# Windowed attention with a gated FFT convolution on one core: gate factors copied out by ScalarE, the inverse's sums as single steps, and an order of work from perturbed priorities

## The chip, the core and the metric

The kernel runs on one core of one Trainium2 chip. The number that counts is the device time of one execution in microseconds; of the kernel before there are three runs, with a median of 190.96 us (190.31 to 191.09). The profile shows one more execution, which took 190.2 us, of which the span from its first to its last instruction is 188.4 us. Engines are named as the profile names them: PE does the matmuls (PEld its weight loads), ACT is ScalarE, DVE is VectorE, POOL is GpSimd, which here issues most of the loads, and SP issues the rest of the loads and all stores.

## The reference

There are 4 batches of 768 positions, 8 heads of width 64, and a model width of 512. The first half is causal attention over a window of 96 positions plus 8 global positions that every row sees, with a linear bias by distance. The second half multiplies two projections of the attention's output with an FFT convolution of a third one.

```python
# attention, for each batch and head
keep   = (pos_k < 8) | ((rel >= 0) & (rel < 96))          # rel = pos_q - pos_k
scores = q @ k.T / 8 - slope[h] * dist                     # dist: rel, or 96 for the global ones
a      = softmax(where(keep, scores, -1e9))
x      = concat_heads(a @ v)                               # 768 x 512
# gate and convolution, for each batch
x1, x2, x3 = split(x @ w_proj, 3)                          # each 768 x 512
conv   = irfft(rfft(x2, axis=0) * rfft(filter, axis=0))    # along the 768 positions
out    = (x1 * conv * x3) @ w_out
```

## The kernel before

**Attention.** Keys lie in 7 tiles of 120 rows with the 8 global rows in front of each. `transposes` brings q and k into the layout that the matmuls want (tiles `QT`, `KT`; line 714, copied out at line 386). The 7 key tiles are worked in 3 chunks c = 0, 1, 2. `scores` makes one chunk's scores for a pair of heads (line 751), ACT takes the exponential of them from two PSUM banks (line 765, tile `E`, 48 times in all), and DVE multiplies with a mask that holds the bias (line 772). For batch 0 the bias can instead be added by PE, by matmuls of `near` with `slope` ahead of the scores (line 742, one or two for each score matmul); then no mask is multiplied. `NEAR = 3` says that this holds for chunks 0, 1 and 2 of batch 0. `values` multiplies with v (lines 790 and 795), DVE takes the reciprocal of the row sums (`rc`, line 819), and `xn` is the scaled result: either one DVE instruction (line 814) or 8 or 12 small ACT instructions (line 818). `transpose_x` turns it into `xT` (line 835).

**Gates.** `gate(b, j, s)` makes 128 columns j of one half s of x1 and x3 for batch b: 8 matmuls into two banks (line 873). The first bank is copied out and scaled to fp16 (tile `x`, line 390 on ACT or 392 on DVE); DVE then multiplies the second bank, still fp32 in PSUM, with it (tile `g`, line 881). There are 32 gates.

**Convolution.** `butterfly` folds x along the positions on DVE (`xab`, `xcf`, `xo`, `xr`, lines 849 to 860), `conv` projects (line 922, copied out to `ab`), transforms (line 700, copied out to `X`), multiplies with the filter's spectrum (`prod`, lines 1039 to 1046), and transforms back (lines 944 and 947, copied out to `eo`, line 386). `mixed` then makes three sums in place on DVE, five instructions (lines 988 to 992) as one step of the plan; `gated` joins the halves (lines 1009, 1010) and multiplies by the gate (line 1014, tile `y`); the last projection is line 970 and its copy-out `ot`.

**What sets the order.** Nothing is issued as the code stands. Each step is recorded in a `Plan` with a cost for each engine that may run it, its reads and writes, and the PSUM banks it takes. `schedule` then plays the steps out once: again and again it takes the step that can start first by the plan's costs, and between steps that can start within 0.03 of each other the one with the smaller key, which is the step's batch, its place in the batch and a bias. Where a step may run on ACT or DVE, the one that ends it first by the costs gets it. The result is a fixed order for each engine; on the chip each engine goes through its own list in that order and waits where a semaphore says so. `fill` puts idle matmuls (tile `idle`, line 382) where the plan leaves PE free for long.

```python
key = lambda o: o.batch[0] + o.batch[1] * o.tail / (total[o.batch] or 1.0) + o.bias
```

Of the kernel before, what the change touches and what calls it, by code (L numbers as in the profile page):

```python
# [13 lines left out]
Alu = mybir.AluOpType  # L14
# [12 lines left out]
def act(n):  # L27
    return 0.06 + n / 1200.0
# [31 lines left out]
class Op:  # L60
    __slots__ = ("cost", "fn", "preds", "succs", "wait", "tail", "bias", "acq", "use", "n",
                 "start", "end", "ready", "eng", "bytes", "batch", "table", "name", "order", "first", "landed")


class Plan:
# [54 lines left out]

    def schedule(self):
        for o in self.ops:
            for x in o.preds:
                x.succs.append(o)
            o.ready = 0.0
        self.before = {}
# [5 lines left out]
        for o in self.ops:  # L132
            o.first = set()
            for b in o.acq:
                for u in b.users:
                    o.first |= self.outer(u, {o}, o)
            o.first -= o.preds | {o}
            o.wait = len(o.preds) + len(o.first)
        after = {}
        for o in self.ops:  # L140
            for x in o.first:
                after.setdefault(x, []).append(o)
        total = {}
        for o in self.ops:
            o.tail = total.get(o.batch, 0.0)
            total[o.batch] = o.tail + o.cost.get("P", 0.0)
        free = {e: BEGIN for e in "PAVGS"}
        banks = [0.0] * 8
# [3 lines left out]
        out = []  # L152
        key = lambda o: o.batch[0] + o.batch[1] * o.tail / (total[o.batch] or 1.0) + o.bias
        while live:
            best = None
            for o in live:
                at = o.ready
                where = None
                if o.acq:
                    if len(o.acq) == 2:  # L160
                        i = min(range(0, 8, 2), key=lambda i: max(banks[i], banks[i + 1]))
                        where = (i, i + 1)
                    else:
                        first = max(at, min(banks))
                        where = [max((i for i in range(8) if banks[i] <= first),
                                     key=lambda i: (banks[i ^ 1], banks[i], -i), default=0)]
# [5 lines left out]
                got = (s, key(o), o, e, where)  # L172
# [37 lines left out]
        self.span = max(o.end for o in out)  # L210
        return self.program(self.fill(out))

    BUSY = 0.225
    FAVOUR = 0.0

# [77 lines left out]
class Fused:  # L293
    PERIOD = 40.0
    NEAR = 3
    LATER = ()
# [251 lines left out]
    def distances(self):  # L548
# [33 lines left out]
        for half in range(2):  # L582
            for k in range(2):
                src, dst = dg[64 * k:64 * k + 64], near[64 * half:64 * half + 64, k]

                def spread(e, src=src, dst=dst):
                    self.copy(e, dst[:, 0:n], src[:, 0:n])
                    self.copy(e, dst[:, n:2 * n + 48], src)
                g.op("AV", {"A": act(216) + act(264), "V": dve(216, 4) + dve(264, 4)}, spread,
                     r=["dg"], w=[("near", half, k)], bias=-2900, name="near")  # L590
# [4 lines left out]
        for half in range(2):  # L595
            ps = slice(64 * half, 64 * half + 64)
            for hp in range(4):
                dst = self.slope[ps, hp].rearrange("p k c -> p (k c)")
                dst = dst[:, 0:256].rearrange("p (k c) -> p k c", k=2)
                for k in range(2):  # L600
                    g.op("AV", {"A": act(64), "V": dve(64, 2)}, lambda e, ps=ps, hp=hp, k=k: self.times(
                        e, self.slope[ps, hp, k, 64 * k:64 * k + 64], self.ident[ps, ps],
                        self.slopes[2 * hp + ps.start // 64] / self.scale),
                        r=["ident", "slope"], w=[("slope", half, hp, k)], bias=-2950, name="slope")

    def masks(self):
        g, nc, NL, n = self.g, self.nc, self.NL, 216
        v, dg, far, mask = nc.vector, self.dg, self.far, self.mask
        for hp in range(4):
# [13 lines left out]
            g.op("V", 2 * dve(400, 4) + 2 * dve(216, 4), spread, r=["far"] + [  # L623
                ("mask", h, at) for h in (2 * hp, 2 * hp + 1) for at in (n, 600)],
# [150 lines left out]
    def values(self, j, c, slot):  # L775
# [34 lines left out]
        def scaled(e):  # L810
# [5 lines left out]
            for i in range(2):  # L816
                for n in range(2 * nt):
                    nc.scalar.mul(to[:, i, n], o[:, i, n, 0:D], rc[:, i, n])  # L818
        g.op("V", 0.09 + 0.05 * nt, lambda _: nc.vector.reciprocal(rc, view()[:, :, :, D:D + 1]),
             use=bs, w=[key], name="rc")  # L820
        g.op("AV", {"A": 4 * nt * act(D), "V": dve(4 * nt * D, 1, True)}, scaled, use=bs, r=[key],
             w=[("xn", j, c)], name="xn")
# [40 lines left out]
    def gate(self, b, j, s):  # L863
# [4 lines left out]
        for o in (0, 2 * self.DM):  # L868
            bk = g.bank()

            def run(_, o=o, bk=bk):
# [8 lines left out]
             use=[pts[0]], w=[key], name="x1")  # L880
        g.op("V", dve(h, 1, True), lambda _: nc.vector.tensor_mul(  # L881
            gt[:, j, h * s:h * s + h], pts[1].f32()[:, 0:h], x1), use=[pts[1]], r=[key],
            w=[("g", b % 2, j, s)], name="g")

# [97 lines left out]
    def mixed(self, js):  # L982
# [3 lines left out]

        def run(_):
            v.tensor_sub(t, z, u)
            v.tensor_scalar(u, u, 2.0, None, op0=Alu.mult)
            v.tensor_add(z, z, u)  # L990
            v.tensor_sub(u, t, w)
            v.tensor_add(w, t, w)
        self.g.op("V", 4 * dve(512 * n, 2) + dve(512 * n, 4), run, name="mix", w=[
            ("mixed", jp) for jp in js] + [
            ("eo", jp, jj, par) for jp in js for jj in range(2) for par in range(2)])

    def gated(self, b, jps, half):
# [8 lines left out]
        def join(_):  # L1006
# [4 lines left out]
        ys = [("y", jp, half) for jp in jps]  # L1011
        g.op("V", dve(512 * n, 2) + dve(256 * n, 2), join, r=[("mixed", jp) for jp in jps] + [
            ("eo", jp, jj, par) for jp in jps for jj in range(2) for par in range(2)], w=ys, name="half")
# [69 lines left out]
    def first_rows(self, vt):  # L1083
# [4 lines left out]
        rows = vt[0:NG, :, :, 0:self.D]  # L1088
        self.g.op("AV", {"A": act(512), "V": dve(512, 2)}, lambda e: self.copy(e, rows[:, 0], st),
                  r=[("X", 0)], w=[("vng", 0, 0, 0)], name="vfirst")  # L1090
# [93 lines left out]
```

## Time and profile before

| what | value |
|---|---|
| median of 3 runs | 190.96 us (190.31 to 191.09) |
| the profiled execution: time, span | 190.2 us, 188.4 us |
| granted PE clock | 1.00 |
| PE busy | 174.0 us, 92% of the span |
| DVE busy | 166.1 us, 88% |
| ACT busy | 144.0 us, 76% |
| POOL busy, all of it before 90 us | 76.6 us, 41% |
| DMA | 20.47 MB |

Three engines are busy most of the time, so the shares alone don't say which one counts. They have to be read stage by stage, and together with the chain of waits. "Busy" counts an instruction from its start to its end: on ACT and DVE the next one often starts before the last has ended, so the step from start to start, called pitch here, is what one more instruction costs. A pitch is read from a row that holds several instructions.

### The profile page before, as it was taken

What the parts mean: (1) busy time and instruction counts of PE and PEld (TensorE: products, weight loads), DVE (VectorE), ACT (ScalarE), POOL (GpSimd) and SP (SyncE); (2) the same over time, 40 slices, a digit from 0 to 9 for tenths busy, and PEclk for the clock granted to TensorE, in tenths of its full rate; (3) what the DMA queues carried; (4) which work ended last, traced back from release to release, by engine and by line L of the source; (5) the groups of instructions that cost most, each with busy time, mean ns of one, the idle gap of its engine ahead of it and who ended that gap; (6) DMA issues with size and microseconds to landing.
All of it is one profiled execution on the core that took longest, in us unless ns stands there. A gap on an engine that the chain in (4) does not pass through costs nothing.

```text
span 188.4 us, 4561 instructions
## 1 busy us (share of the span) xinstructions
PE 174.0 (92%) x1742; PEld 105.7 (56%) x1742; DVE 166.1 (88%) x378; ACT 144.0 (76%) x292; POOL 76.6 (41%) x97
## 2 busy tenths in 40 slices
PE   7877999999899999899898999999998999999891
PEld 2345886656445667575355567754466675447440
DVE  6898875998999969999997869999999999999960
ACT  7389983568999999988967669859869576588352
POOL 8799993599989999993000000000000000000000
PEclk9999999999999999999999999999999999999999
DMA  6999999999999999999053000000260000005244
GB/s 134 197 167 149 153 196 209 154 153 152 143 171 145 154 141 140 142 151 132 4 220 117 0 3 0 3 0 2 80 257 1 5 0 0 3 29 194 111 165 169
DMA packets 90916, 20.47 MB, mean 109 GB/s; under 512 B 83816, under 2 KB 87824, under 8 KB 90896
## 3 DMA queue, kind: packets, MB, share of 16 engines
q0 software_dynamic: 80912, 12.14, 95.6%
q1 hardware_dynamic: 9984, 8.06, 13.6%
q8 instruction: 13, 0.21, 0.5%
q14 instruction: 7, 0.06, 0.1%
HBM read 25.84 MB, written 6.29 MB: 171 GB/s over the span
## 4 chain that ended last, share of the span: by engine, by line
DVE 42%; PE 32%; ACT 13%; issue 4%; SPq 4%; DMA 3%; DVEq 0%; ACTq 0%
PE bank L873 13%; PE bank L970 5%; DVE E L772 4%; SPq L402 4%; DVE g L881 4%; ACT E L765 4%; DMA ot<-in_q_dram 3%; DVE xn L814 3%; DVE y L1014 3%; PE bank L922 2%; PE bank L944 2%; DVE pp L1039 2%; ACT xn L818 2%; ACT QT L386 2%; PE bank L790 2%
## 5 line engine op out<-in xcount | busy, mean ns | idle before, releaser
L873 PE MATMUL bank<-xT,w 128*128 128x384 f16 x256 | 45.0, 326 | 0.2 <-ACT xT L386 0.2
L765 ACT ACTIVATE E<-bank 128x864 f16<-128x864 f32 x48 | 40.1, 910 | 1.2 <-PE bank L751 0.6
L873 PEld LDWEIGHTS <-w 128*128 128x128 f16 x256 | 24.3, 98 | 16.3 <-issue 1.3
L402 POOL DMA_DIRECT2D kn<-in_k_dram x28 | 26.6, 960 | 0.7 <-issue 0.5
L402 POOL DMA_DIRECT2D vn<-in_v_dram x28 | 25.6, 928 | 2.5 <-DMA w<-in_moe_w_proj_dram 1.9
L390 ACT ACTIVATE x<-bank 128x384 f16<-128x384 f32 x29 | 14.7, 508 | 12.7 <-PE bank L873 10.5
L970 PE MATMUL bank<-wo,y 128*128 128x512 f16 x96 | 21.9, 379 | 1.1 <-DVE y L1014 1.0
L772 DVE TENSOR_TENSOR E<-E,mask 128x864 f16<-128x864 f16 x36 | 20.5, 594 | 1.2 <-ACT E L765 1.1
L881 DVE TENSOR_TENSOR g<-bank,x 128x384 f16<-128x384 f32 x32 | 17.1, 549 | 3.9 <-PE bank L873 3.6
L390 ACT ACTIVATE ot<-bank 128x512 f32<-128x512 f32 x21 | 12.5, 597 | 8.2 <-PE bank L970 8.1
L402 POOL DMA_DIRECT2D qn<-in_q_dram x18 | 16.2, 910 | 5.0 <-DMA g<-in_moe_filter_fft_dram 3.5
L751 PE MATMUL bank<-QT,KT 64*128 64x216 f16 (+2 forms) x224 | 15.8, 241 | 2.0 <-ACT E L765 0.9
L970 PEld LDWEIGHTS <-y 128*128 128x128 f16 x96 | 9.0, 98 | 13.1 <-DVE y L1014 3.1
L790 PE MATMUL bank<-vn,E 128*128 128x65 f16 x224 | 15.5, 193 | 0.9 <-ACT E L765 0.8
L814 DVE TENSOR_TENSOR xn<-bank,rc 128x512 f16<-128x512 f32 (+1 forms) x21 | 16.1, 771 | 0.2
L390 ACT ACTIVATE ab<-bank 128x512 f16<-128x512 f32 x21 | 12.5, 611 | 4.0 <-PE bank L922 3.9
L790 PEld LDWEIGHTS <-E 128*128 128x128 f16 x224 | 14.0, 97 | 2.6 <-DVE E L772 0.7
L795 PE MATMUL bank<-vn,E 128*128 128x65 f16 x192 | 15.2, 193 | 0.0
L386 ACT CAST eo<-bank 128x384 f16<-128x384 f32 x29 | 12.9, 509 | 1.7 <-PE bank L947 1.2
L751 PEld LDWEIGHTS <-KT 64*128 64x128 f16 x224 | 8.5, 94 | 9.2 <-issue 5.8
L386 ACT CAST X<-bank 128x512 f16<-128x512 f32 x21 | 11.9, 606 | 2.2 <-PE bank L700 2.1
L795 PEld LDWEIGHTS <-E 128*128 128x128 f16 x192 | 13.2, 97 | 0.6 <-issue 0.3
(141 smaller groups left out, 361.6 us busy)
## 6 DMA issues: line engine op xcount, KB each, us to landing
out_dram<-ot SPq DMA_DIRECT2D x24, 256.0 KB, 2.6
kn<-in_k_dram POOLq DMA_DIRECT2D x28, 120.0 KB, 6.0
vn<-in_v_dram POOLq DMA_DIRECT2D x28, 120.0 KB, 6.7
qn<-in_q_dram POOLq DMA_DIRECT2D x18, 128.0 KB, 6.7
ot<-in_q_dram SPq DMA_DIRECT2D x6, 256.0 KB, 5.8
w<-in_moe_w_proj_dram POOLq DMA_DIRECT2D x4, 256.0 KB, 6.6
g<-in_moe_filter_fft_dram POOLq DMA_DIRECT2D x1, 768.0 KB, 11.9
w<-in_moe_w_proj_dram POOLq DMA_DIRECT2D x1, 512.0 KB, 8.6
```

What stands on the lines that cost most here:

```text
L386: {"A": nc.scalar.copy, "V": nc.vector.tensor_copy, "G": nc.gpsimd.tensor_copy}[e](out, in_)
L390: self.nc.scalar.mul(out, in_, c)
L402: return self.g.op(eng, 0.57 + 0.00035 * nbytes[0] if eng == "G" else 0.5, lambda _: e.dma_start(dst, src), w=w, r=r, nbytes=nbytes, name= ...
L751: nc.tensor.matmul(bs[hh].f32()[:, off:off + w], self.KT[hs, hp, P * m:P * m + P], self.QT[hs, hp, KL * m:KL * m + w], start=(off == 0 and ...
L765: g.op("A", act(864), lambda _: nc.scalar.activation(eo, bs[0].two()[:, :, 0:432].rearrange("p h (m w) -> p h m w", m=2), Act.Exp, scale=s ...
L772: g.op("V", dve(864, 2), lambda _: nc.vector.tensor_mul(eo, eo, mk), r=[("E", hp, gi), ("mask", hp)], w=[("E", hp, gi)], name="masked")
L790: nc.tensor.matmul(o[:, n, hh], ef[:, at:at + P], vt[:, t, 2 * hp + hh, :], start=first, stop=(t == 0), skip_group_check=True)
L795: nc.tensor.matmul(o[:, n, hh], ef[:, at:at + P], vt[:, t - 1, 2 * hp + hh, :], start=False, stop=True, skip_group_check=True)
L814: nc.vector.tensor_mul(to, o[:, :, :, 0:D], rc.to_broadcast([P, 2, 2 * nt, D]))
L873: nc.tensor.matmul(bk.f32()[:, 0:h], self.w[:, c, o + P * j:o + P * j + P], self.xT[:, c, h * s:h * s + h], start=(c == 0), stop=(c == 3))
L881: g.op("V", dve(h, 1, True), lambda _: nc.vector.tensor_mul(gt[:, j, h * s:h * s + h], pts[1].f32()[:, 0:h], x1), use=[pts[1]], r=[key], w ...
L970: nc.tensor.matmul(bk.f32(), y[:, c, P * t:P * t + P], self.wo[:, c, :], start=(c == 0), stop=(c == 3))
```

## The change

- **Gates.** For all 32 gates (`TWICE`) ACT copies the second bank, x3, out to fp16 in the tile `g` (new line 920); DVE then multiplies `g` with x1 from SBUF to SBUF (new line 922).
- **The inverse's sums.** The five instructions of `mixed` are five steps of the plan, so that other DVE work can be put between them, and `gated` waits for the three that it reads.
- **`NEAR` is 2.** Chunk 2 of batch 0 gets its bias by the mask on DVE and no longer by PE.
- **Costs.** Some costs in the plan are other numbers: the casts of q, `near`, the mask's `spread`, `rc`, and `xn` on ACT (4 x 0.2 for each tile in place of 4 x 0.113). The copies of `slope` are for ACT alone.
- **Order.** Before the play-out, 25 seeds each shift the key of some steps by a random amount (`noise`) and their leaning towards ACT or DVE (`lean`).

```diff
     def schedule(self):
+        self.prepare()
+        for seed in self.SEEDS:
+            self.shake(seed)
+        return self.program(self.fill(self.lay()))
+
+    def shake(self, seed):
+        r = random.Random(seed)
+        if r.random() < 0.4:
+            groups = sorted({(o.name, o.batch) for o in self.ops if o.eng not in "GS"})
+            g, by = r.choice(groups), r.gauss(0.0, 5.0)
+            lean = r.gauss(0.0, 0.3)
+            for o in self.ops:
+                if (o.name, o.batch) == g:
+                    o.noise += by
+                    o.lean += lean
+            return
+        share = r.choice((0.005, 0.02, 0.05))
+        for o in self.ops:
+            if r.random() < share:
+                o.noise += r.gauss(0.0, 5.0)
+                o.lean += r.gauss(0.0, 0.3)
...
+            o.rank = o.batch[0] + o.batch[1] * o.tail / (total[o.batch] or 1.0) + o.bias + o.noise
...
-                           key=lambda x: (x[1] + o.cost[x[0]] + self.FAVOUR * (x[0] == "V"), x[0]))
+                           key=lambda x: (x[1] + o.cost[x[0]] + o.lean * (x[0] == "V"), x[0]))
...
+    SEEDS = (4, 6, 12, 14, 28, 33, 52, 54, 91, 94, 109, 172, 179, 217, 284, 340, 370, 416, 512,
+             1076, 1771, 1829, 3912, 4133, 4161)
...
-    NEAR = 3
+    NEAR = 2
+    TWICE = frozenset((b, j, s) for b in range(4) for j in range(4) for s in range(2))
...
-            self.g.op("AV", {"A": act(512), "V": dve(512, 2)}, lambda e: self.copy(
+            self.g.op("AV", {"A": act(512), "V": 0.7}, lambda e: self.copy(
...
-                    g.op("AV", {"A": act(64), "V": dve(64, 2)}, lambda e, ps=ps, hp=hp, k=k: self.times(
+                    g.op("A", {"A": 0.145}, lambda e, ps=ps, hp=hp, k=k: self.times(
...
-        g.op("AV", {"A": 4 * nt * act(D), "V": dve(4 * nt * D, 1, True)}, scaled, use=bs, r=[key],
+        g.op("AV", {"A": 4 * nt * 0.2, "V": dve(4 * nt * D, 1, True)}, scaled, use=bs, r=[key],
...
+        x3, ko = gt[:, j, h * s:h * s + h], ("g", b % 2, j, s)
+        if (b, j, s) in self.TWICE:
+            g.op("A", act(h), lambda _: nc.scalar.copy(x3, pts[1].f32()[:, 0:h]), use=[pts[1]],
+                 w=[ko], name="x3")
+            g.op("V", dve(h, 2), lambda _: nc.vector.tensor_mul(x3, x3, x1), r=[key], w=[ko], name="g")
+            return
...
-        def run(_):
-            v.tensor_sub(t, z, u)
-            v.tensor_scalar(u, u, 2.0, None, op0=Alu.mult)
-            v.tensor_add(z, z, u)
-            v.tensor_sub(u, t, w)
-            v.tensor_add(w, t, w)
...
+        op(lambda _: v.tensor_sub(t, z, u), (), "mt")
+        op(lambda _: v.tensor_scalar(u, u, 2.0, None, op0=Alu.mult), ("mt",), "mu", 4)
+        op(lambda _: v.tensor_add(z, z, u), ("mt", "mu"), "mz")
+        op(lambda _: v.tensor_sub(u, t, w), ("mt", "mu", "mz"), "m1")
+        op(lambda _: v.tensor_add(w, t, w), ("mt", "m1"), "m2")
```

How the instructions move is shown at three places, word for word from the built programs' orders. Line numbers of the changed kernel are 37 to 42 higher; `bank` with a number is a pair of PSUM banks.

**ACT at the start, up to the first exponentials.** `ot` here holds the loaded rows of q in fp32, and `ot_104` the last of the six tiles. Before:

```order
L612 ACTIVATE mask<-dg 128x48
L612 ACTIVATE mask<-dg 128x216
L386 CAST qn<-ot_103 128x512
L386 COPY QT<-bank_122 128x4x128
L386 CAST qn<-ot_104 128x512
L765 ACTIVATE E_67<-bank_123 128x2x2x216
L765 ACTIVATE E_68<-bank_124 128x2x2x216
```

Now:

```order
L423 CAST qn<-ot_102 128x512
L423 COPY QT<-bank_121 128x4x128
L649 ACTIVATE mask<-dg 128x48
L423 CAST qn<-ot_103 128x512
L423 COPY QT<-bank_121 128x4x128
L802 ACTIVATE E_68<-bank_123 128x2x2x216
L802 ACTIVATE E_67<-bank_124 128x2x2x216
```

The cast of the sixth tile of q no longer stands ahead of the exponentials (it is DVE's), while four other casts that DVE had are ACT's.

**ACT at the first gates of batch 0.** Before:

```order
L390 ACTIVATE x_95<-bank_123 128x384
L390 ACTIVATE x_96<-bank_121 128x384
L390 ACTIVATE x_97<-bank_122 128x384
L390 ACTIVATE x_98<-bank_123 128x384
L494 ACTIVATE y<-bank_123 128x512
```

Now (`g_87 <- bank` is the new copy of x3):

```order
L427 ACTIVATE x_95<-bank_124 128x384
L427 ACTIVATE x_96<-bank_122 128x384
L920 CAST g_87<-bank_123 128x384
L427 ACTIVATE x_97<-bank_123 128x384
L920 CAST g_87<-bank_124 128x384
L920 CAST g_87<-bank_122 128x384
L920 CAST g_87<-bank_121 128x384
```

Seven copies stand where four were, and the pair of banks of a gate is freed by ACT alone.

**DVE at the end of batch 2's inverse**, where the fold for batch 3 is made as well. Before:

```order
L856 TENSOR_TENSOR xo<-xab,xcf 128x1024
L988 TENSOR_TENSOR mix<-eo 128x1024
L989 TENSOR_SCALAR eo<-eo 128x8x128
L990 TENSOR_TENSOR eo<-eo 128x8x128
L991 TENSOR_TENSOR eo<-mix,eo 128x8x128
L992 TENSOR_TENSOR eo<-mix,eo 128x8x128
```

Now:

```order
L1033 TENSOR_TENSOR mix<-eo 128x1024
L886 TENSOR_TENSOR xab<-xT 128x1536
L888 TENSOR_TENSOR xab<-xT 128x1536
L1034 TENSOR_SCALAR eo<-eo 128x8x128
L891 TENSOR_TENSOR xcf<-xab 128x1024
L892 TENSOR_TENSOR xcf<-xab 128x1024
L1035 TENSOR_TENSOR eo<-eo 128x8x128
L893 TENSOR_TENSOR xo<-xab,xcf 128x1024
L1036 TENSOR_TENSOR eo<-mix,eo 128x8x128
```

The five sums stood back to back, each touching a tile that the one ahead of it reads or writes; now work of the fold stands between them.

More of the change, by code (lines that the diff above doesn't have):

```diff
@@ L61 @@
     __slots__ = ("cost", "fn", "preds", "succs", "wait", "tail", "bias", "acq", "use", "n",
-                 "start", "end", "ready", "eng", "bytes", "batch", "table", "name", "order", "first", "landed")
+                 "start", "end", "ready", "rank", "noise", "lean", "need", "eng", "bytes", "batch", "table", "name", "order", "first", "landed")
 class Plan:
@@ L124, in schedule @@
                 x.succs.append(o)
-            o.ready = 0.0
+            o.noise, o.lean = 0.0, self.FAVOUR
+            o.eng = next(iter(o.cost))
         self.before = {}
@@ L137, in schedule @@
             o.first -= o.preds | {o}
-            o.wait = len(o.preds) + len(o.first)
-        after = {}
+            o.need = len(o.preds) + len(o.first)
+        self.after = {}
         for o in self.ops:
             for x in o.first:
-                after.setdefault(x, []).append(o)
+                self.after.setdefault(x, []).append(o)
         total = {}
@@ L146, in schedule, with lay @@
             total[o.batch] = o.tail + o.cost.get("P", 0.0)
+        self.total = total
+    def schedule(self):
+        self.prepare()
[18 more added lines that the diff above has]
+                o.lean += r.gauss(0.0, 0.3)
+    def lay(self):
+        for o in self.ops:
+            o.wait, o.ready = o.need, 0.0
+            for b in o.acq:
+                b.left, b.free = 1 + len(b.users), 0.0
+        total, after = self.total, self.after
         free = {e: BEGIN for e in "PAVGS"}
@@ L152, in schedule @@
         out = []
-        key = lambda o: o.batch[0] + o.batch[1] * o.tail / (total[o.batch] or 1.0) + o.bias
+        for o in self.ops:
+            o.rank = o.batch[0] + o.batch[1] * o.tail / (total[o.batch] or 1.0) + o.bias + o.noise
         while live:
@@ L985, in mixed, with op @@
         z, u, w = (eo[:, :, :, P * m:P * m + P] for m in range(3))
-        def run(_):
[L988 to L995, printed above, removed]
+        def op(fn, r, w, rate=2):
+            self.g.op("V", dve(512 * n, rate), fn, name="mix", r=[("eo", jp, jj, par) for jp in js
+                      for jj in range(2) for par in range(2)] + [(k, jp) for k in r for jp in js],
+                      w=[(w, jp) for jp in js])
+        op(lambda _: v.tensor_sub(t, z, u), (), "mt")
[3 more added lines that the diff above has]
+        op(lambda _: v.tensor_add(w, t, w), ("mt", "m1"), "m2")
     def gated(self, b, jps, half):
```

22 lines of the change are left out of this document (11 added, 11 removed).

## The prediction

> **What bounds the kernel now.** I cut the span at the first projection matmul (line 922) of each batch, which the trace puts at 41.9, 85.5, 127.4 and 156.3 us, and asked for the busy time of each engine in the five stretches: batch 0's attention, three mixed stages, and the end.
>
> ```profile
> 0.00:41.90 41.90, 37.73 (x447) 24.49 (x448) 34.44 (x107) 28.78 (x66) 34.44 (x51) 1.00 1.77 168
> 41.90:85.50 43.60, 41.09 (x451) 26.02 (x449) 40.56 (x91) 41.41 (x85) 41.17 (x46) 1.00 2.46 149
> 85.50:127.40 41.90, 39.97 (x405) 24.16 (x402) 37.27 (x74) 32.76 (x70) 1.00 (x2) 1.00 0.31 52
> 127.40:156.30 28.90, 28.13 (x298) 17.71 (x299) 28.35 (x56) 22.93 (x41) 0.00 (x0) 1.00 0.15 56
> 156.30:188.40 32.10, 27.09 (x149) 13.27 (x146) 25.47 (x56) 18.11 (x35) 0.00 (x0) 1.00 0.26 99
> ```
>
> The columns are length, PE, PEld, DVE, ACT, POOL. The reader sees that PE is busy 94 to 97% in the middle three, DVE 93, 89 and 98%, ACT 95, 78 and 79%. PE's number flatters it, since its ends are modelled; the chain of waits says who really ends last:
>
> ```profile
> DVE 42%; PE 32%; ACT 13%; issue 4%; SPq 4%; DMA 3%; DVEq 0%; ACTq 0%
> PE bank L873 13%; PE bank L970 5%; DVE E L772 4%; SPq L402 4%; DVE g L881 4%; ACT E L765 4%; DMA ot<-in_q_dram 3%; DVE xn L814 3%; DVE y L1014 3%; PE bank L922 2%; PE bank L944 2%; DVE pp L1039 2%; ACT xn L818 2%; ACT QT L386 2%; PE bank L790 2%
> L873 PE MATMUL bank<-xT,w 128*128 128x384 f16 x256 | 45.0, 326 | 0.2 <-ACT xT L386 0.2
> ```
>
> DVE carries 42% of it, so a us taken off DVE in the middle is worth most. ACT has room from 85.5 us on, little between 41.9 and 85.5. The kernel is not bound by one engine: whoever gets faster will soon wait for PE.
>
> **The gates.** The rows of the multiplication, of ACT's copies of the same shape (128x384 fp32 in PSUM to fp16), and of DVE sums between two fp16 tiles in SBUF:
>
> ```profile
> 125.29 1.48 DVE L881 TENSOR_TENSOR g<-bank,x 128x384 f16<-128x384 f32 x3
> 153.58 2.95 ACT L386 CAST eo<-bank 128x384 f16<-128x384 f32 x7 [0.44 <-PE bank L947]
> 177.05 0.42 DVE L1009 TENSOR_TENSOR y<-eo 128x512 f16<-128x512 f16 x1
> 177.39 0.28 DVE L1010 TENSOR_TENSOR y<-eo 128x256 f16<-128x256 f16 x1
> 177.59 0.42 DVE L1009 TENSOR_TENSOR y<-eo 128x512 f16<-128x512 f16 x1
> ```
>
> Three multiplications take 1.48 and one alone 0.55, so the pitch is (1.48 - 0.55) / 2 = 0.47. Between SBUF tiles, 512 elements have a pitch of 177.39 - 177.05 = 0.34 and 256 one of 0.20; 384 lie half-way, 0.27. So each gate takes 0.20 off DVE, 32 of them 6.4 us; bounds 0.13 (as the 512 row) and 0.27 (as the 256 row), 4.2 and 8.6. ACT pays (2.95 - 0.49) / 6 = 0.41 a gate, 13.1 us. By the Trainium skill's cycle table ("VectorE: DVE Perf Modes", the errata section: 58 cycles and half the elements for SBUF, 120 and all of them for PSUM) I estimate 0.27 a gate, 8.5 us in all; the rows' pitches say less and stand.
>
> **`xn` goes back to DVE.** ACT did it three times in 28 small instructions, as these rows show, and now never:
>
> ```profile
> 41.90:85.50 43.60, 2.59 (x12) 1.00 2.46 149
> 85.50:127.40 41.90, 3.39 (x16) 1.00 0.31 52
> 100.05 3.39 ACT L818 ACTIVATE xn<-bank,rc 128x64 f16<-128x64 f32 x16 [1.10 <-DVE rc L819]
> 99.97 0.69 DVE L814 TENSOR_TENSOR xn<-bank,rc 128x512 f16<-128x512 f32 x1
> 100.58 0.20 DVE L819 RECIPROCAL rc<-bank 128x8 f32<-128x8 f32 x1
> 103.76 0.41 DVE L386 COPY xT<-bank 128x480 f16<-128x480 f16 x1 [1.11 <-PE bank L835]
> ```
>
> ACT saves 6.0 us. DVE pays three times 0.61 (100.58 - 99.97), with a larger one for 12 columns, 2.1 in all. At 100 us the 3.39 us stand on the chain (its row is "ACT xn L818 2%"), and DVE has idle time just there; two DVE instructions do the same in 1.2. I take 1.2 of the possible 2.2 as won.
>
> **Other moves between ACT and DVE**, counted in the two orders: DVE loses 4 `KT`, 3 casts of q, 2 `ab`, 1 `ot`, 1 `inr`, 5 `slope`; it gains 3 `xT`, 1 `X`, 1 `eo`, 2 `x`. At pitches of 0.3 to 0.6 these are about -2 us for DVE and +3 for ACT. With 4 masks more (0.52 each, +2.1) and the gates, DVE is down by 6.4 - 2.1 + 2 - 2.1 = 4.2 us, ACT up by 13.1 - 6.0 + 3 = 10 us.
>
> **The sums as single steps.** Before, one group of them with the work behind it:
>
> ```profile
> 122.05 0.68 DVE L988 TENSOR_TENSOR mix<-eo 128x1024 f16<-128x1024 f16 x1
> 122.77 0.43 DVE L989 TENSOR_SCALAR eo<-eo 128x1024 f16<-128x1024 f16 x1
> 123.23 0.69 DVE L990 TENSOR_TENSOR eo<-eo 128x1024 f16<-128x1024 f16 x1
> 123.96 0.69 DVE L991 TENSOR_TENSOR eo<-mix,eo 128x1024 f16<-128x1024 f16 x1
> 124.68 0.69 DVE L992 TENSOR_TENSOR eo<-mix,eo 128x1024 f16<-128x1024 f16 x1
> 126.69 0.68 DVE L854 TENSOR_TENSOR xcf<-xab 128x1024 f16<-128x1024 f16 x1
> 127.29 0.68 DVE L855 TENSOR_TENSOR xcf<-xab 128x1024 f16<-128x1024 f16 x1
> 172.98 0.41 DVE L988 TENSOR_TENSOR mix<-eo 128x512 f16<-128x512 f16 x1
> ```
>
> A sum that the next one waits for steps on after 0.72 (122.05 to 122.77), an independent one of the same shape after 0.60 (126.69 to 127.29). Four such waits a group are 0.5 us. With other work between, as the orders show for the large groups, it is gone: 3 x 0.5 = 1.5. The two last, half as large, run from 172.98 to 177.05, 4.07 us, where eight pitches of 0.34 and two of about 0.22 would be 3.2; interleaved with each other they save 0.9. Bounds: nothing (the time between is only filled with DVE work that came earlier anyway) and 2.4.
>
> **The start.** Two things stand on its chain:
>
> ```profile
> 14.14 0.62 ACT L386 CAST qn<-ot 128x512 f16<-128x512 f32 x1 [0.85 <-DMA ot<-in_q_dram]
> 14.67 3.23 ACT L765 ACTIVATE E<-bank 128x864 f16<-128x864 f32 x4
> 17.76 0.61 ACT L386 COPY QT<-bank 128x512 f16<-128x512 f16 x1
> 23.66 0.55 PE L742 MATMUL bank<-near,slope 64*128 64x216 bf16 x12
> 24.05 0.35 PE L751 MATMUL bank<-QT,KT 64*128 64x216 f16 x6
> 95.48 1.63 DVE L772 TENSOR_TENSOR E<-E,mask 128x864 f16<-128x864 f16 x3
> 27.02 5.36 PE L873 MATMUL bank<-xT,w 128*128 128x384 f16 x32
> 2.59 1.82 ACT L390 ACTIVATE slope<-ident 64x64 bf16<-64x64 f16 x11 [0.36 <-DVE slope L594]
> 6.82 0.70 DVE L386 CAST qn<-ot 128x512 f16<-128x512 f32 x1
> 12.49 3.15 POOL L402 DMA_DIRECT2D kn<-in_k_dram  x3
> ```
>
> The first exponentials stand behind the cast of q's sixth tile, which waits 0.85 for its load; without it they can start 0.85 and the cast's 14.67 - 14.14 earlier, 1.4 us. The four groups of 12 `near` matmuls that go away take 24.05 - 23.66 = 0.4 each, 1.6 us of PE; four masks on DVE come instead, at a pitch of (1.63 - 0.60) / 2 = 0.52, where DVE was busy 34.4 of 41.9. Against both stands ACT: in this stretch it gets 8 copies of x3 (3.3), 3 casts (1.6), 5 `slope` (0.17 each, 0.8), and by its order also the tables `inv` and `inr`, which came after the first `ab` before (about 2 us). That is 7.7 on 28.8. It can't begin in earnest before the first tile of q is there at 6.8, and does only the `slope` copies (2.7) till then, so 4 us are lost at the front: 40.6 of 41.9, with every wait for PE still to come. So the 3 us are mostly eaten: I take -0.5, between -3.0 and +2.0. The 2 us of tables are work taken out of the next stage, where ACT was 95% busy. On POOL's queue the second load of v for chunk 1 goes behind three loads of k, 3.15 us; ahead of `w` stand the same loads as before. I cost this at nothing, since the values of chunk 1 also wait for exponentials; were these early, up to 3 us would show, which the +2.0 and the gain of 1.4 beside it cover.
>
> **The sum.** Gate multiplications (line 881) in the middle three stages:
>
> ```profile
> 41.90:85.50 43.60, 4.79 (x10) 1.00 2.46 149
> 85.50:127.40 41.90, 3.69 (x7) 1.00 0.31 52
> 127.40:156.30 28.90, 1.15 (x3) 1.00 0.15 56
> ```
>
> Start -0.5. Middle three stages: DVE's gates there are 20, by the rows below, -4.0; the sums -1.5; the other evacuations -1.0; `xn` +2.1; so DVE has 4.4 us less. I count 3/4 of it, since PE is the next to end last, which is -3.2; and -1.2 for the chain through `xn` at 100 us, but only half of it beside the first, -0.6. The end: the two interleaved groups -0.9, the gates that stand between there save 0.2 each but one more of them is put at the very end, -0.1; -1.0 in all. Together -5.3 us. The profiled execution took 190.2 us (span 188.4), 0.8 below the median of 190.96; against the median the forecast is 185.7.
>
> **Rivals.** *More of the same* (chance 0.14): all of DVE's time is on the path and the start wins its 3 us: -3.0 - 4.4 - 1.2 - 1.0 = -9.6, 181.4. For it: DVE's 42% of the chain. Against: ACT's 40.6 of 41.9 in the first stretch.
>
> *PE is the bound* (0.10): it is busy 109.2 of 114.4 us in the middle. Then DVE's time was only cover, and what counts is the 1.6 of PE's own work at the start, of which ACT's fuller first stretch eats 1.0: 190.4, no change. Against it: gate matmuls step on after 5.36 / 32 = 0.167, half of the 0.33 that one is shown to last, so the ends of such rows count as busy what is only latency.
>
> *ACT holds the gates' banks* (0.09): both banks of a gate are now freed by ACT, whose queue holds exponentials of 0.77 (14.67 to 17.76 for four), `X`, `ab` and copies. Each time a copy of x3 stands behind one, PE's next gate waits for a bank. PE needs 8 x 0.167 = 1.3 for a gate, ACT 0.8. Where an exponential comes between every two gates, a gate takes ACT 1.2, still under 1.3; where two come, 1.6, and PE loses 0.3. If 24 of 32 gates lose 0.3, that is 7.2 us against 5.3 won: slower by 1.9, 192.9. It decides from 5.3 / 32 = 0.17 lost per gate on. For it: ACT's 41.4 of 43.6 in the second stretch. Against: `xn`'s 2.6 and `inv`'s 1.9 leave that stretch, and about 10 copies of x3 (4.1) come. The Trainium skill speaks for this rival ("VectorE: DVE Perf Modes", Rules for kernel authors): for elementwise work on a matmul's output, accept the PSUM rate or copy it out first if there are many operations on it; here there is one. In this trace's pitches the pair costs 0.41 + 0.27 where 0.47 was, so by that rule 32 gates would lose 6.7 us of engine time; the trace gives it that sum, and denies only that ACT's time is the time that counts after 85.5 us.
>
> *The order is worse than it plans* (0.03): the shifts suit the plan's costs, not the chip, and one engine's list waits for 2 us in each of four stages: +8 against -5.3, 193.4. Nothing in the profile of before can speak to it.
>
> **Chances.** The forecast keeps 0.64. Faster by over 0.5% is this with the first rival, less 0.01 for its upper edge: 0.77. That bound, 0.95 us, is about what a measurement of this kernel can tell from no change, its runs lying 0.4% apart. No change: 0.10 and that 0.01, 0.11. Slower: 0.09 + 0.03 = 0.12. The range reaches up to the case of no change, 190.3, and down to 182.3, where DVE's 4.4, the 1.2, the end and 2.1 of the start's 3.0 count; outside it I leave the slower cases and half of the first rival.
>
> **What would show it.** In the profile after: `g` on DVE at 0.27 pitch and no ACT `xn`; first exponentials near 13.3 us; the first projection matmul between 40 and 43; the middle from first to last projection near 110 us where it was 114.4; ACT busy near 154, DVE near 161. Wrong would be: idle time of PE's gates ended by ACT, a first projection after 44 us, or a middle that stays at 114.

## The result and the profile after

The changed kernel takes 183.34 us (median of 182.06, 182.92, 183.77 and 185.39), the kernel before on the same chip 190.7: a ratio of 0.9592, 95% interval 0.9529 to 0.9655, or 7.4 us less by the medians. The forecast was 185.7 us, within 182.3 to 190.3. All ratios here compare undisturbed runs only, while a median may include disturbed ones, and three profiles below are of disturbed executions (without shuffles 189.1 us, sums together 192.4, steps alone 192.7), which is why a few medians, ratios and stages below do not quite fit each other. The profiled execution took 182.9 us with a span of 181.1.

The page of the changed kernel: busy time by engine, TensorE's granted clock in 40 slices, and the shares of the chain of work that ended last, by engine and by line (the gate matmuls are L910 now, the output projection L1012, the projections L964), and the row of the gate matmuls, whose last number is the idle time ahead of them.

```profile
PE 170.5 (94%) x1693; PEld 104.6 (58%) x1693; DVE 160.4 (89%) x376; ACT 154.1 (85%) x305; POOL 76.5 (42%) x97
...
PEclk9997899999999999999999999999999999999998
...
PE 73%; DMA 11%; ACT 7%; POOL 4%; issue 2%; DVE 1%; POOLq 0%; ACTq 0%
PE bank L910 20%; PE bank L1012 12%; PE bank L964 10%; DMA qn<-in_q_dram 7%; PE bank L737 5%; PE bank L751 5%; PE bank L986 5%; PE bank L788 4%; DMA kn<-in_k_dram 4%; PE bank L872 3%; PE bank L827 3%; ACT E L802 3%; PE bank L832 2%; POOL vn L439 1%; ACT h L427 1%
...
L910 PE MATMUL bank<-xT,w 128*128 128x384 f16 x256 | 43.9, 326 | 0.0
```

Before, that chain was DVE 42%, PE 32%. Now it is PE 73% and DVE 1%. DVE lost 5.7 us of busy time and ACT gained 10.1. The chain names the last to end, though; the experiments show that DVE's time still counts.

The stages, cut as before at each batch's first projection matmul (busy time of PE, PEld, DVE, ACT, POOL, then granted clock, DMA share, GB/s):

```profile
core 0: us, PE busy (x) PEld busy (x) DVE busy (x) ACT busy (x) POOL busy (x), PEclk, DMA share, GB/s
0.00:43.30 43.30, 38.62 (x413) 24.65 (x414) 34.81 (x107) 37.30 (x90) 33.27 (x50) 0.96 1.97 163
43.30:83.20 39.90, 38.14 (x425) 24.51 (x423) 38.84 (x86) 36.74 (x68) 37.41 (x42) 1.00 2.46 145
83.20:121.10 37.90, 37.55 (x396) 23.18 (x394) 35.02 (x73) 34.04 (x63) 5.78 (x7) 1.00 0.62 74
121.10:151.80 30.70, 30.66 (x326) 19.17 (x324) 28.89 (x60) 27.02 (x51) 0.00 (x0) 1.00 0.14 53
151.80:181.10 29.30, 25.51 (x145) 13.14 (x142) 22.82 (x55) 18.96 (x37) 0.00 (x0) 0.97 0.28 108
```

The lengths were 41.9, 43.6, 41.9, 28.9 and 32.1 us. So the start is 1.4 longer, the middle three are 3.7 and 4.0 shorter and 1.8 longer, together 5.9 shorter, and the end is 2.8 shorter: 7.3 us of span. PE is busy for 106.4 of the middle's 108.5 us. DVE's busy time in the middle fell by 3.4 us (106.2 to 102.8) and PE's by 2.8, so the 5.9 us gained there are more than either engine was relieved of: both also wait less.

The gate's two rows in the groups of instructions: ScalarE's copy of the second factor, and the multiplication that now reads it from SBUF.

```profile
L920 ACT CAST g<-bank 128x384 f16<-128x384 f32 x32 | 15.7, 496 | 3.2 <-PE bank L910 2.7
L922 DVE TENSOR_TENSOR g<-g,x 128x384 f16<-128x384 f16 x32 | 10.8, 349 | 0.1
```

What the multiplication takes is read from DVE's timeline, by its step to the next row: 31.96 - 31.69 = 0.27 us, where it was 0.47.

```profile
31.69 0.34 DVE L922 TENSOR_TENSOR g<-g,x 128x384 f16<-128x384 f16 x1
31.96 0.59 DVE L809 TENSOR_TENSOR E<-E,mask 128x864 f16<-128x864 f16 x1
```

In the start, ScalarE's first exponentials come at 12.25 us, where they came at 14.67:

```profile
12.25 3.24 ACT L802 ACTIVATE E<-bank 128x864 f16<-128x864 f32 x4
```

They are lost again at once. PE's timeline, with the idle time ahead of a row in brackets, and then the clock by the microsecond:

```profile
14.82 0.19 PE L832 MATMUL bank<-vn,E 128*128 128x65 f16 x1
16.30 0.61 PE L751 MATMUL bank<-ident,kn 128*128 128x128 f16 x4 [1.28 <-DMA kn<-in_k_dram]
```

```profile
15.00:16.00 1.00, 0.02 (x1) 0.00 (x0) 1.00 (x2) 0.49 (x1) 0.25 (x1) 0.82 2.48 148
16.00:17.00 1.00, 0.70 (x7) 0.70 (x8) 0.71 (x4) 0.00 (x0) 0.75 (x1) 0.50 2.40 151
17.00:18.00 1.00, 1.00 (x10) 0.72 (x8) 0.95 (x2) 0.63 (x2) 1.00 (x2) 0.50 2.42 154
18.00:19.00 1.00, 1.00 (x18) 1.00 (x17) 0.53 (x2) 1.00 (x5) 1.00 (x3) 0.50 2.40 162
19.00:20.00 1.00, 1.00 (x19) 0.76 (x17) 1.00 (x6) 0.78 (x4) 1.00 (x2) 0.98 2.38 145
```

PE waits 1.28 us for a load of k. From 15.64 us on (the last 0.36 us of that microsecond at 0.50 make its 0.82) TensorE runs at half clock, until about 19.0: 3.4 us. In the profile of before, the clock was 1.00 throughout. This dip is not in every execution: one run of the changed kernel shows a mean clock of 0.996, where 3.4 us at half clock alone make it 0.991, and it took 182.06 us.

### The profile page after: what moved, and what is told of

The parts are those of the page before. It is cut to its first block, busy times and chain, and to the rows that moved or that the text cites. A ratio compares the mean times of both kernels' runs of the same rounds, so it can differ in the third digit from the quotient of the medians.

```text
span 181.1 us, 4437 instructions
## 1 busy us (share of the span) xinstructions
PE 170.5 (94%) x1693; PEld 104.6 (58%) x1693; DVE 160.4 (89%) x376; ACT 154.1 (85%) x305; POOL 76.5 (42%) x97
## 3 DMA queue, kind: packets, MB, share of 16 engines
q0 software_dynamic: 80912, 12.14, 106.4%
## 4 chain that ended last, share of the span: by engine, by line
PE 73%; DMA 11%; ACT 7%; POOL 4%; issue 2%; DVE 1%; POOLq 0%; ACTq 0%
PE bank L910 20%; PE bank L1012 12%; PE bank L964 10%; DMA qn<-in_q_dram 7%; PE bank L737 5%; PE bank L751 5%; PE bank L986 5%; PE bank L788 4%; DMA kn<-in_k_dram 4%; PE bank L872 3%; PE bank L827 3%; ACT E L802 3%; PE bank L832 2%; POOL vn L439 1%; ACT h L427 1%
## 5 line engine op out<-in xcount | busy, mean ns | idle before, releaser
L910 PE MATMUL bank<-xT,w 128*128 128x384 f16 x256 | 43.9, 326 | 0.0
L802 ACT ACTIVATE E<-bank 128x864 f16<-128x864 f32 x48 | 41.4, 919 | 0.8 <-PE bank L788 0.4
L910 PEld LDWEIGHTS <-w 128*128 128x128 f16 x256 | 24.2, 98 | 15.4 <-DVE xT L423 0.2
L439 POOL DMA_DIRECT2D kn<-in_k_dram x28 | 25.8, 927 | 11.6 <-PE bank L751 11.4
L809 DVE TENSOR_TENSOR E<-E,mask 128x864 f16<-128x864 f16 x40 | 23.1, 596 | 0.5 <-ACT E L802 0.5
L1012 PE MATMUL bank<-wo,y 128*128 128x512 f16 x96 | 21.9, 379 | 0.0
L851 DVE TENSOR_TENSOR xn<-bank,rc 128x512 f16<-128x512 f32 (+1 forms) x24 | 18.3, 770 | 0.3
L920 ACT CAST g<-bank 128x384 f16<-128x384 f32 x32 | 15.7, 496 | 3.2 <-PE bank L910 2.7
L827 PE MATMUL bank<-vn,E 128*128 128x65 f16 x224 | 16.1, 195 | 1.7 <-ACT E L802 1.1
L427 ACT ACTIVATE ab<-bank 128x512 f16<-128x512 f32 x23 | 14.0, 613 | 2.8 <-PE bank L964 2.8
L427 ACT ACTIVATE x<-bank 128x384 f16<-128x384 f32 x27 | 13.7, 513 | 3.1 <-PE bank L910 2.7
L832 PE MATMUL bank<-vn,E 128*128 128x65 f16 x192 | 15.6, 194 | 0.0
L1012 PEld LDWEIGHTS <-y 128*128 128x128 f16 x96 | 9.2, 98 | 10.7 <-DVE y L1056 0.6
L423 ACT CAST eo<-bank 128x384 f16<-128x384 f32 x28 | 12.0, 513 | 2.8 <-PE bank L989 2.6
L419 PE MATMUL bank<-idle 128*128 128x512 f16 x37 | 11.9, 452 | 1.2 <-DVE idle L490 1.2
```

What stands on the lines that cost most here:

```text
L427: self.nc.scalar.mul(out, in_, c)
L439: return self.g.op(eng, 0.57 + 0.00035 * nbytes[0] if eng == "G" else 0.5, lambda _: e.dma_start(dst, src), w=w, r=r, nbytes=nbytes, name= ...
L802: g.op("A", act(864), lambda _: nc.scalar.activation(eo, bs[0].two()[:, :, 0:432].rearrange("p h (m w) -> p h m w", m=2), Act.Exp, scale=s ...
L809: g.op("V", dve(864, 2), lambda _: nc.vector.tensor_mul(eo, eo, mk), r=[("E", hp, gi), ("mask", hp)], w=[("E", hp, gi)], name="masked")
L827: nc.tensor.matmul(o[:, n, hh], ef[:, at:at + P], vt[:, t, 2 * hp + hh, :], start=first, stop=(t == 0), skip_group_check=True)
L832: nc.tensor.matmul(o[:, n, hh], ef[:, at:at + P], vt[:, t - 1, 2 * hp + hh, :], start=False, stop=True, skip_group_check=True)
```

## The experiments

First four on where the gain comes from.

**The changed kernel without its shuffles.**

```diff
-    SEEDS = (4, 6, 12, ..., 3912, 4133, 4161)
+    SEEDS = ()
```

> The changed kernel without the 25 shuffles of the scheduler's priorities; all other edits stay. Theory (DVE's shorter gates and the sums as single steps are what counts, PE ends last now): at most 1.5 us of the 7.4 goes back, 183 to 185 us. Rival (the searched order itself is what counts, the shorter operations are only its material): 4 us or more go back, 187 to 189 us.

Ratio to before 0.9771 (0.9717 to 0.9824), median 187.83. Of the 4.1% some 2.3 are there without the search and 1.8, about 3.4 us, come with it. That lies between the two expectations (by the medians it would be 4.5 us, inside the rival's); neither the order nor the operations carry it alone.

**Other seeds.**

```diff
-    SEEDS = (4, 6, 12, ..., 3912, 4133, 4161)
+    SEEDS = tuple(range(20001, 20026))
```

> The changed kernel with 25 other seeds, not chosen by anything. Theory (the order matters little, DVE's relief is the gain): within 2 us of the kernel without shuffles, 183 to 186 us. Rival (the choice of the seeds is the gain): 187 to 190 us, as without shuffles or worse.

Ratio 0.979 (0.9762 to 0.9818), median 186.64: as without shuffles. No gain from shuffling by itself is seen; choosing the shuffles brings one. The time falls between the two expectations' numbers, and both allowed that it would be as without shuffles; the 2.0% to the changed kernel speak for the rival.

**Slow gates in the same order.**

```diff
+            def slow(_):
+                nc.vector.tensor_copy(x1, x1)
+                nc.vector.tensor_mul(x3, x3, x1)
-            g.op("V", dve(h, 2), lambda _: nc.vector.tensor_mul(x3, x3, x1), r=[key], w=[ko], name="g")
+            g.op("V", dve(h, 2), slow, r=[key], w=[ko], name="g")
```

> The order of the changed kernel is kept row by row on every engine, and each gate multiplication gets a copy of x1 onto itself ahead of it on DVE (f16, 128x384, about 0.2 us), so that a gate costs DVE again what it cost before, while ScalarE still releases both banks. 32 x 0.2 = 6.4 us more on DVE, 20 of the 32 in the middle stages (4.0). Theory (DVE's relief is the gain): 2.5 to 5 us slower than the changed kernel, 186 to 188 us. Rival (the order is the gain, DVE has room in it): less than 1.5 us slower, 183.5 to 185 us.

194.36 us, ratio 1.0199 (1.0168 to 1.0229): 11.0 us slower than the changed kernel by the medians, 11.6 by the ratios, beyond both expectations. DVE's timeline at one of the gates:

```profile
47.79 0.54 DVE L923 COPY x<-x 128x384 f16<-128x384 f16 x1
48.44 0.36 DVE L924 TENSOR_TENSOR g<-g,x 128x384 f16<-128x384 f16 x1
48.71 0.68 DVE L674 TENSOR_TENSOR g<-pp 128x1024 f16<-128x1024 f16 x1
49.31 0.40 DVE L423 COPY KT<-bank 128x480 f16<-128x480 f16 x1
...
50.23 0.61 DVE L423 COPY KT<-KT 128x224 f16<-128x224 f16 x1
```

The dose was mis-sized. From a copy's start to the multiplication's start it is 48.44 - 47.79 = 0.65 us here, 0.28 to 0.36 in the gates after 114 us, when POOL issues no loads any more; over the 32 gates it adds up to 12.6 us, not 6.4. So 11.0 / 12.6 = 0.87 of DVE's extra time arrives in the end (0.92 by the ratios). That is no even rate: 6.5 us of the delay fall on the second stage of the profile (46.4 us where it was 39.9). How, is seen at 48 us in PE's waits, and in stretches of 2 us:

```profile
PE bank L788 <- DVE KT L423: 3.0, 1, 3.0
```

```profile
48.00:50.00 2.00, 0.00 (x0) 0.00 (x0) 1.90 (x5) 0.55 (x1) 1.99 (x4) 1.00 2.43 143
50.00:52.00 2.00, 1.10 (x12) 0.72 (x12) 1.97 (x6) 0.49 (x1) 2.00 (x3) 0.55 2.96 115
52.00:54.00 2.00, 2.00 (x10) 0.96 (x9) 1.78 (x5) 1.99 (x3) 2.00 (x3) 0.50 1.37 190
54.00:56.00 2.00, 2.00 (x9) 0.37 (x7) 1.81 (x4) 1.34 (x3) 1.42 (x3) 0.50 2.20 160
56.00:58.00 2.00, 1.99 (x22) 0.75 (x21) 1.19 (x5) 1.50 (x2) 1.83 (x3) 0.74 2.41 153
```

The copy of KT stands on DVE's list behind two of the slow gates (49.31 and 50.23 above). PE waits 3.0 us for it and runs at half clock from 50.2 to 57.0 us, which loses it 3.4 us of work. PE goes through its list in order, so one late row on DVE cost its delay and here the clock on top. Without these 3.4 us the share would be about 0.6 (an estimate: 7.6 of 12.6).

**The sums together in the same order.** The five steps of each group stand back to back at the place of the first; PE's and ScalarE's rows are the same.

```diff
-        return self.program(self.fill(self.lay()))
+        out = self.fill(self.lay())
+        for group in self.sums:
+            at = min(out.index(o) for o in group)
+            for o in group:
+                out.remove(o)
+            out[at:at] = group
+        return self.program(out)
```

> The order of the changed kernel, but the five sums of each group stand back to back on DVE again, at the place of the group's first; PE's and ScalarE's rows stay as they are. The first four groups move past 4 to 10 rows, at the end the two groups stand one after the other again. Theory (the single steps are worth the 1.5 + 0.9 us of the prediction): 1.5 to 2.5 us slower than the changed kernel, 185 to 186 us. Rival (what the steps let by, one or two evacuations of 0.3 to 0.5 us, is not waited for, and only the pitch of the last two groups counts): 0 to 1 us slower.

Ratio 0.9964 (0.9932 to 0.9996): 0.037 of 190.7, 7 us slower than the changed kernel, which no theory had. PE's longest wait in it and another one, and the clock around the first:

```profile
PE bank L916 <- DVE xT L429: 2.7, 1, 2.7
...
PE bank L970 <- DVE xcf L897: 1.8, 1, 1.8
```

```profile
80.00:82.00 2.00, 0.14 (x3) 0.00 (x0) 1.90 (x4) 0.59 (x2) 2.00 (x3) 1.00 1.87 118
82.00:84.00 2.00, 1.14 (x4) 0.58 (x5) 1.97 (x4) 0.00 (x0) 2.00 (x3) 0.57 2.26 144
84.00:86.00 2.00, 2.00 (x8) 0.95 (x7) 0.66 (x1) 1.33 (x3) 2.00 (x3) 0.58 2.24 141
```

At 79 to 82 us four of the sums now stand ahead of the copy of `xT` on DVE, and the gate matmuls wait 2.7 us for it. PE has 0.14 of 2 us busy, then 3.4 us at half clock (2 x 0.86 + 2 x 0.84, from the 0.57 and 0.58). The stage came to 44.9 us against 39.9. The fourth stage is 2.2 longer (32.9 against 30.7), with a wait for DVE's `xcf` of 1.8 us at 159 us. At the end, where the two groups no longer interleave, the last stage is 30.2 against 29.3: that 0.9 is the prediction's. The clock is the smaller part: one run with a granted clock of 1.00 took 189.1 us, still 5.7 above the changed kernel's median. The profiled start is 1.3 longer too, without any of these sums in it.

Then two on PE's share.

**One more matmul per gate, after and before.** The same edit in both kernels:

```diff
+                if not o:
+                    nc.tensor.matmul(bk.f32()[:, 0:h], self.w[:, 0, P * j:P * j + P],
+                                     self.xT[:, 0, h * s:h * s + h], start=True, stop=True)
                 for c in range(4):
```

> The changed kernel with the first matmul of each gate's x1 factor done twice: 32 x 0.167 = 5.3 us more on PE, nothing else. Theory (after the change PE ends last, 73% of the chain): 4 to 5.5 us slower than the changed kernel, 187.5 to 189 us. Rival (DVE still sets the time): at most 2 us slower, 185 us.

> The kernel before with the same 5.3 us more on PE. Theory (PE 32% and DVE 42% of the chain before, so PE has room): 1 to 2.5 us slower, 192 to 193.5 us. Rival (PE counts in full in both, and the change did not shift what ends last): 4 to 5.5 us slower, 195 to 196 us.

After: 187.87 us, ratio 0.9807 (0.9764 to 0.9849), 2.15% of before above the changed kernel, 4.1 us (2.6 to 5.6 with both intervals), or 0.77 of the 5.3. Before: ratio 1.0105 (1.0059 to 1.0152), 2.0 us (1.1 to 2.9), 0.38 of it. The chain by engine, of the changed kernel with the matmul and of the kernel before with it:

```profile
PE 74%; DMA 8%; DVE 8%; POOL 3%; ACT 3%; issue 2%; POOLq 0%; ACTq 0%; DVEq 0%
```

```profile
PE 42%; DVE 34%; ACT 13%; SPq 4%; DMA 3%; issue 3%; ACTq 0%; DVEq 0%
```

Both came as the theory had it. PE's time counts about twice as much after the change, though the two intervals overlap a little; with DVE's 0.87, neither engine has much room left in this order.

Two on the start.

**Idle matmuls in the wait.**

```diff
+        ks = [o for o in line if o.name == "k"][2]
+        ...
+        d.fn = lambda _, b=b: self.busy(6, b)
+        line.insert(line.index(ks), d)
         return line
```

> The changed kernel with six idle matmuls (128x512, 1.3 us in all) put on PE's queue where it waits 1.28 us for a load of k at 15.0 us; nothing else is moved. Theory (the 3.4 us at half clock behind that wait are paid for with PE's time): the granted clock stays at 1.00 from 15 to 20 us and the time falls by 1 to 1.7 us, to 181.5 to 182.5 us. Rival (the start waits for loads anyway): no change, 183 us, or 0.5 us more where the load lands early.

182.84 us, ratio 0.9544 (0.9501 to 0.9586). The same stretch by 2 us:

```profile
14.00:16.00 2.00, 1.77 (x20) 0.96 (x17) 2.00 (x4) 1.27 (x2) 1.75 (x3) 1.00 2.53 149
16.00:18.00 2.00, 1.93 (x38) 1.59 (x36) 1.79 (x7) 1.51 (x6) 2.00 (x3) 1.00 2.39 153
18.00:20.00 2.00, 2.00 (x36) 1.44 (x34) 2.00 (x7) 2.00 (x6) 2.00 (x4) 1.00 2.67 149
```

The clock stays at 1.00, and the first projection comes at 42.2 instead of 43.3; the rest takes 138.1 us, where 181.1 - 43.3 = 137.8 was. That the filled wait keeps the clock up is seen in the trace; the gain of about 1 us in the time is not shown, since the two intervals overlap. By its ratio it is the fastest kernel here, within that noise.

**k ahead of v.** In the list of the same order one load changes its place:

```diff
+        v, k = at["load('vn', 0)3"], at["load('kn',)3"]
+        out.remove(v)
+        out.insert(out.index(k) + 1, v)
```

> The changed kernel with one load moved on POOL's queue: the fourth tile of v goes behind the two loads of k for the second chunk, which are issued 0.9 us earlier. Theory: PE's wait of 1.28 us shrinks to 0.4, the clock stays at 1.00, the stage to the first projection gets 1.5 to 2.5 us shorter, 181 to 182 us. Rival (the first projection is set by the loads of w and of the next q, which stay where they are): 183 us.

183.3 us, ratio 0.9572 (0.9533 to 0.9611): no change, as the rival's number had it. PE's waits show why:

```profile
PE bank L756 <- DVE qn L428: 1.2, 1, 1.2
...
PE bank L832 <- DMA vn<-in_v_dram: 1.1, 1, 1.1
PE bank L832 <- DVE vn L428: 1.0, 2, 0.6
```

The wait for k is gone, and PE waits for DVE's cast of q and for v instead; the clock dips all the same, from 16.6 to 20 us. Behind the load stood a cast, and then the next load.

Last, the parts alone, in the kernel before.

**Copies, steps, and both.** ScalarE's copy and the multiplication from SBUF are put into the kernel before, as in the change's diff, and nothing else; so are the five single sums; then both. The scheduler lays the list anew for each.

> The kernel before with ScalarE's copy of the second gate factor for all 32 gates, and nothing else of the change. Theory (6.4 us less on DVE, which carried 42% of the chain, against 13 us more on ScalarE): 1.5 to 4 us faster than before, 186.5 to 189 us. Rival (ScalarE holds the gates' banks and is as full as DVE was): no gain or up to 2 us slower, 190 to 193 us.

> The kernel before with the last sums as five single steps, and nothing else of the change. Theory (1.5 us in the middle and 0.9 at the end, as the prediction has it, half of it to be seen without the rest): 0.5 to 1.5 us faster, 189 to 190 us. Rival (the scheduler's list puts them back to back again): no change, 190.7 us.

> The kernel before with the copies and the single steps together; no shuffles, three chunks of the first batch with `near` as before. Theory (these two carry all that the search does not): like the changed kernel without shuffles, ratio 0.975 to 0.985, 186 to 188 us. Rival (the parts only work in the changed kernel's own order): 189 to 191 us.

Copies alone: ratio 1.0059 (1.0024 to 1.0094), slower by 1.1 us. Steps alone 0.9976 (0.9944 to 1.0009), both 0.9989 (0.9958 to 1.002): no change. The rivals' numbers held all three times, but not each reason: with the steps alone the list does not put them back to back again (in the first group one other instruction stands between the third and the fourth sum and one between the fourth and the fifth, in the second group up to six), and they gain nothing all the same. Each of these is one list from the scheduler; how far another list of the same operations moves the time was tried in the changed kernel alone (0.9771 and 0.979). In the kernel with the copies alone, the rows of ScalarE's copy and who waited for them; its `xn` on ScalarE; and the second stage:

```profile
L882 ACT CAST g<-bank x32: 458/478/614, 30.1 to 164.1; 128x384 f16<-128x384 f32 x32
...
who waited for it (us, times):
  DVE g L884: 4.7, 6
```

```profile
L818 ACT ACTIVATE xn<-bank,rc x24: 306/336/376, 60.1 to 143.7; 128x64 f16<-128x64 f32 x24
```

```profile
43.44:88.38 44.94, 41.65 (x455) 26.23 (x453) 41.91 (x99) 41.55 (x82) 39.13 (x44) 1.00 2.44 143
```

DVE waits 4.7 us for copies that stand late in ScalarE's queue; in the changed kernel nothing waits for them. In the whole of this kernel ScalarE still does 24 of the `xn`, 8 of them in this stage, and it is busy 41.6 of 44.9 us, in a stage that took 43.6 before. In the changed kernel without shuffles, which has no `xn` on ScalarE, the same stage reads

```profile
45.53:87.79 42.26, 39.91 (x445) 25.31 (x443) 39.87 (x90) 39.37 (x72) 38.75 (x44) 1.00 2.36 137
```

**The search alone.** The kernel before, its operations and planned costs, with 19 shuffles found in the same way (written as the changed kernel with all else set back; the seeds are shown):

```diff
+    SEEDS = (13, 32, 84, 99, 100, 194, 205, 215, 390, 713, 745, 959, 1059, 1327, 1434, 1717, 1843,
+             2480, 2736)
```

> The kernel before, its operations and planned costs unchanged, with the same kind of search over the priorities: shuffles with seeds from 0 to 4161, each kept if the planned end comes earlier, 19 kept. Theory (the order is what moves the time, and copies and single steps add the smaller part): 3 to 5 us faster than before, ratio 0.974 to 0.985, 186 to 188 us. Rival (the search only pays with the shorter gates and the single steps to place): less than 1.5 us faster, ratio above 0.992.

Ratio 0.9796 (0.9745 to 0.9846), median 187.55: 2.0%, 3.9 us. The theory held. The search is worth about as much without the rest of the change (2.0%, 1.5 to 2.6) as with it (1.8%, about 1.0 to 2.6).

## Why the prediction was right, and where it was not

The sign, the range and the size within 2.4 us were right, and of what was to be seen nearly all came: `g` at 0.27, no `xn` on ScalarE, ACT 154.1 for 154, DVE 160.4 for 161, the middle at 108.5 for 110; the first projection at 43.3 lay just outside 40 to 43. The split was not right: the start missed by 1.9 us one way, the middle (-5.9 for -3.8) and the end (-2.8 for -1.0) by 2.1 and 1.8 the other, so that the sum came as near as it did is in part luck.

**A term is missing: the order itself.** The prediction read the shifts of priorities only as a risk (its last rival, 0.03, +8 us). The search is 1.8 to 2.0% by two comparisons, 3.4 to 3.9 us, about half of the result. The rows of before could have hinted at it: with PE busy 109.2 of 114.4 in the middle and DVE ending the chain, how the list fits two nearly full engines together mattered.

**The term "DVE has 4.4 us less, I count 3/4" was given to the wrong edits.** (3/4 of 4.4 is 3.3, not 3.2.) In the changed kernel's order the share is not far off (0.87 by the slow gates, about 0.6 without the clock's part). But the copies of x3 and the single sums, which gave that term its -4.0 and -1.5, bring nothing when they are put into the kernel before (0.9989). The other 2.2% between that and the changed kernel without shuffles (0.9771) came with what else differs there: `near` for two chunks instead of three, and the planner's corrected costs, which take `xn` off ScalarE and `slope` to it. The prediction had booked the corrected costs of `xn` as 2.1 us more on DVE, against 0.6 won on the chain. It may be that the copies pay only once `xn` has left ScalarE: the second stage is 2.7 us shorter without it. But that stage also holds other work (445 matmuls for 455), and costs and `near` were not run apart, so the cause of the 2.2% stays open.

**The start, -0.5, came as +1.4.** The exponentials came even earlier than said (12.25 for 13.3). The step that failed is the one costed at nothing: the loads of v and k that change places on POOL's queue. It looked for trouble at a v load behind k, and the wait was for k, 1.28 us, behind a v load moved ahead; the half clock after it was not foreseen at all. Of the 1.9 us missed, filling the wait gives back 1.1 in the profiles; moving that v load back behind k gives back nothing. ScalarE's work was forecast well (28.8 + 7.7 = 36.5, measured 37.3), but of the 4 us it was to lose at the front it lost 1.7 (busy 5.06 of the first 6.8). It was full only from 20 to 42 us (20.7 of 22), and PE's waits for its exponentials come to 1.8 us in the whole kernel; what its fullness costs the start was not tried.

**The end, -1.0, came as -2.8.** The 0.9 for the two interleaved groups was measured at 0.9. The other 1.8 us appear only in the changed kernel's order: the last stage is 31.9 without the shuffles and with the other seeds, and 31.7 with the search alone. What in the order brings them was not looked for.

**Rivals.** ScalarE held no banks of note in the changed kernel, as forecast (the gate matmuls have 0.0 us of idle time ahead of them); it did delay the copies where they were put in alone. The Trainium skill's rule in "VectorE: DVE Perf Modes", Rules for kernel authors, that a single operation on a matmul's output should take the PSUM rate rather than a copy first, agrees with that run: 1.1 us slower. In the changed kernel it is not followed, and there extra time on DVE cost 0.87 of itself. PE did become the next bound: 0.77 of its added time counts, 0.38 before.

## What to carry to other kernels

Where two engines are each busy for nine tenths, an edit that shortens operations can be worth nothing by itself, and a search over the order may be worth as much as the edits; time the order alone and the edits alone before giving either the credit. To ask what an engine's time is worth, add a known dose to it in a frozen order, and read from the trace how large the dose really was. Look at the granted clock behind TensorE's waits of over a microsecond: some of them here were paid twice, as idle time and as half clock, and idle matmuls put into one of them kept the clock up.

## What the hardware showed that was not expected

The granted clock can fall to 0.50 after short gaps. After 1.28 us idle (with gaps of 0.40 and 0.33 shortly before) it stayed there for 3.4 us, after 3.0 us idle for 6.8. The length of one gap does not decide it: a gap of 1.08 us in the changed kernel with one more matmul per gate was followed by a dip of 3.4 us, while 1.77 us with the sums together (at 159 us), 1.25 with the other seeds (at 12 us) and 1.18 with the search alone (at 52 us) were not. What decides it was not tried. The Trainium skill, in "TensorE: Matmul & The Clock Gate", Part 1, puts the halving after at least one idle window of about 3.4 us; the length of the dips agrees with that window, the gaps that set them off here are shorter.

In the slow gates, a copy of 128x384 f16 and the start of the multiplication behind it took 0.28 to 0.36 us in the 22 gates where POOL was issuing no load meanwhile. In the ten where it was, seven took 0.47 to 0.71 and three 0.35 to 0.39. That the two are cause and effect was not tried.
